# Who makes the sums over k1 beside the convolution: VectorE or GpSimd

## Chip, core and metric

The kernel runs on one core of a Trainium2 chip. The metric is the device time of one execution in microseconds. Engines are named as in the profile: PE (TensorE, matmuls), PEld (its weight loads), DVE (VectorE), ACT (ScalarE), POOL (GpSimd), SP (SyncE, which issues most DMAs).

## What is computed

Two blocks follow each other: a long convolution by FFT with a gate, and a maxout FFN.

```python
h_mlp = np.maximum(pos_emb @ w1, 0.0) @ w2          # filter, S x D
h_filt = h_mlp * np.exp(-0.01 * pos)[:, None]
u = x * v                                           # 4 x 12544 x 128
Uf, Hf = np.fft.rfft(u, n=2*S, axis=1), np.fft.rfft(h_filt, n=2*S, axis=0)
y = np.fft.irfft(Uf * Hf[None], n=2*S, axis=1)[:, :S]
a = x * y                                           # as 50176 tokens x 128
h = np.maximum(np.maximum(a @ moe_w1, a @ moe_w2), a @ moe_w3)   # d_ff 768
return h @ moe_w_out
```

## The kernel before

The FFT over 2S points is written as matmuls with constant tables: a first transform over 90 values of k1, a second stage per pair of k1 (group g, 45 of them), the product with the filter's spectrum, the inverse second stage (back to DRAM, `zd`), and a last transform over k1 that gives y. The FFN works with the differences w2-w1 and w3-w1, so that two relu-like maxima and one folded matrix `lin` give the maxout.

**Passes, tiles and slots.** After a first part that convolves batch 0, there are four FFN passes, one per batch b. Pass b runs over 32 tiles i of 392 tokens; a tile has six slots f, one per 128 columns of d_ff. Slot number s = 6i + f. In each slot `up` (L155 into `hps`, L702 on ACT, L705 on DVE) makes one piece of h, and `down` (L155 into `ops`) of two slots earlier multiplies it by `wo_sb`. `hps` has three PSUM banks in strict turns, and each `up` takes two, so the bank read by L705 of slot s is the one that slot s+2 writes first: L705 has to end by then.

**What is woven in.** Passes 0, 1 and 2 carry the convolution of batch b+1. `conv_steps` lays it out: first the input's transforms (u steps, slots 3 to about 55 or 62), then the pairs. For a group x, two groups at a time, there are: `g_quarter` (PE, L463 for the second stage of g=x, L473 for the inverse one of z=x-3), `g_fold` (ACT L485, DVE L488 twice, out of PSUM), `g_store` (POOL DMA, L496), `q_swap` (ACT L503, L504), `q_re` (DVE L507), `q_im` (DVE L512, then POOL L515), and two `q_unfold` (DVE L519), whose result L473 reads three groups later. Fold, swap and store have fixed slots; `q_re`, `q_im` and `q_unfold` go to the slot with the least load in a short list, `load`, among the few that are allowed. Every engine works through its queue in the order in which the program was written.

**The sums over k1.** For the next tile, `t_load` brings `zt` from `zd` on SP, `t_sums` forms even = z0 + z1 (L670) and z1 = z0 - z1 (L671), and `t_last` transforms both on PE (L155 into `cps`, slot f = 2 to 4) and multiplies by x on DVE (L692, `gt`). `t_sums` stands ahead of `up` in slot f = 0. Which engine it uses is decided there: DVE in a pass's last tile, DVE once the pairs have begun (`i * NF > pairs_from`), POOL before. For the upper half of the tiles of passes 1 to 3 a sign is needed, and `t_sums` takes DVE's scalar_tensor_tensor (L674, L675) whatever engine is named. `pairs_from` is s0, 55 in pass 0 and 62 in passes 1 and 2.

```python
if f == (3 if turn_ else 0):
    t_sums(tiles[n + 1], nc.vector if turn_ or i * NF > pairs_from else nc.gpsimd)
```

Outputs leave by a POOL DMA (L720), in the queue behind what POOL has to do before. Pass 3 has no convolution beside it and sums on DVE; POOL adds products there (L735).

Of the kernel before, what the change touches and what calls it, by code (L numbers as in the profile page):

```python
# [28 lines left out]
LATE = 3  # L29
# [61 lines left out]
def kernel(  # L91
# [15 lines left out]
    nc = tc.nc  # L107
# [4 lines left out]
    NF = DFF // P  # L112
    NK = N1 // 2
# [459 lines left out]
    def conv_steps(b, done):  # L573


        out = []

        def at(slot, late, fn, *args):
            out.append((slot, late, len(out), fn, args))

        per_pair = 170 / (NK + LATE + 0.6 * (NU - done))
        for u in range(done, NU):
            s = (u - done) * 0.6 * per_pair + 9
            at(max(0, int(s) - 9), 0, u_load, b, u)
            at(int(s) - 6, 0, u_mul, u)
            at(int(s) - 5, 0, u_planes, u)
            at(int(s) - 4, 0, u_dma, u)
            at(int(s), 0, u_join, u)  # L590
            at(int(s + 1), 1, u_first, u)
        s0 = int((NU - done - 1) * 0.6 * per_pair + 9) + 6

        def start(x):
            return s0 + int(x // 2 * 2 * per_pair)

        load = [(1.2 if i % NF == 3 else 0.6) + (1.4 if i % NF == 0 and i > s0 else 0)
                for i in range(NT * NF)]
        for x in range(NK + LATE):
            s = start(x)  # L600
            load[s] -= 1.2
            load[s + 1 + x % 2] += 1.4

        def emptiest(among, cost):
            s = min(among, key=lambda i: load[i])
            load[s] += cost
            return s

        for x in range(NK + LATE):
            s, odd = start(x), x % 2  # L610
            g, z = x if x < NK else None, x - LATE if x >= LATE else None
            at(s, 1, g_quarter, g, z)
            at(s + 1 + odd, 0, g_fold, g, z)
            at(s - 4, 0, w_load, x)
            if z is not None:
                at(s + 3 + odd, 0, g_store, b, z)
            if g is None:
                continue
            if g % 2 == 0:
                at(s - 4, 0, q_load, g, min(2, NK - g))  # L620
                at(s - 1, 0, h_load, g, min(2, NK - g))
            first = s + 2 + 2 * odd
            at(first, 0, q_swap, g, 0)
            at(first + 1, 0, q_swap, g, 64)
            last = start(x + LATE) - 1
            a = emptiest(range(first + 1, min(first + 3, last - 1) + 1), 0.7)
            at(a, 0, q_re, g)
            a = emptiest(range(a, min(first + 4, last - 1) + 1), 0.7)
            at(a, 0, q_im, g)
            for q in range(2):  # L630
                at(emptiest(range(a + 1, last + 1), 0.55), 0, q_unfold, g, q)
        slots = {}
        for s, _, _, fn, args in sorted(out, key=lambda r: r[:3]):
            slots.setdefault(s, []).append((fn, args))
        return slots, {start(x) + 1 for x in range(NK + LATE)}, s0


    N = 4 * NB
    NT = P // 4
    zts, xTs, gs, pos_, obs = ({} for _ in range(5))  # L640

    def t_load(b, i):
        zt = hp.tile([N1, 2, 512], FP32, tag="zt", name="zt", bufs=2)
        for c in range(2):
            if b == 0:
                nc.sync.dma_start(
                    zt[NK * c:NK * c + NK],
                    zd[b].rearrange("(g a) c t f -> g a c t f", a=2)[
                        :, :, c, 2 * i:2 * i + 2, :].rearrange("g a t f -> g a (t f)"))
                continue  # L650
            q, j = divmod(i, NT // 2)
            for a in range(2):
                nc.sync.dma_start(
                    zt[NK * c:NK * c + NK, a].rearrange("g (t f) -> g t f", t=2),
                    zd[b].rearrange("(g a) c t q f -> g a c t q f", a=2)[
                        :, a, c ^ (a & q), 2 * j:2 * j + 2, q, :])
        zts[b, i] = zt[:, 0], zt[:, 1]
        if i % 2:
            return
        xT = hp.tile([D, 2, 4, NB], FP32, tag="xT", name="xT", bufs=2)  # L660
        for c in range(GC):
            nc.sync.dma_start(xT[c * NG:(c + 1) * NG].rearrange("d i p n -> d (i p) n"),
                              x[:, 4 * i:4 * i + 8, c, b, :])
        xTs[b, i], xTs[b, i + 1] = xT[:, 0], xT[:, 1]

    def t_sums(i, eng=nc.gpsimd):
        z0, z1 = zts[i]
        even = hp.tile([N1, 512], FP32, tag="even", name="even", bufs=2)
        if i[0] == 0 or i[1] < NT // 2:
            eng.tensor_tensor(out=even[:], in0=z0, in1=z1, op=ALU.add)  # L670
            eng.tensor_tensor(out=z1, in0=z0, in1=z1, op=ALU.subtract)  # L671
        else:
            for out, op in ((even[:], ALU.add), (z1, ALU.subtract)):
                nc.vector.scalar_tensor_tensor(out=out, in0=z1, scalar=sign_t[:, 0:1], in1=z0,  # L674
                                               op0=ALU.mult, op1=op)  # L675
        zts[i] = even[:], z1

    def t_last(i):
        zt = zts.pop(i)
        ps = state["bank"]()  # L680
        own = i[0] == B - 1 and i[1] > 1
        g = (lp if own else hp).tile([D, 4, NB], FP32, tag="g", name="gt", bufs=4 if own else 3)
        y = ps[:, 0:N].rearrange("d (p n) -> d p n", p=4)

        h = NB // 2
        for s in range(4):
            for a in range(2):
                halves_mm(y[:, s, a * h:a * h + h], zt[a][:, s * D:(s + 1) * D],
                          f4p[:, i[0] > 0 and i[1] >= NT // 2, a, :], s == 0 and a == 0, True)
        y = y.rearrange("d p (a m) -> d p m a", a=2)  # L690
        xT = xTs.pop(i)
        nc.vector.tensor_tensor(out=g[:].rearrange("d p (m a) -> d p m a", a=2), in0=y,  # L692
                                in1=xT.rearrange("d p (m a) -> d p m a", a=2),
                                op=ALU.mult)
        gs[i] = g

    def up(i, f, tag="hid", bufs=3):
        rhs = gs[i][:].rearrange("d p n -> d (p n)")
        h = (hidp if tag == "hid" else lp).tile([P, N], FP32, tag=tag, name="hid", bufs=bufs)
        pa = next(hbanks)  # L700
        halves_mm(pa[:, 0:N], w_sb[1][:, f * P:(f + 1) * P], rhs, True, True)
        nc.scalar.activation(h[:], pa[:, 0:N], Relu)  # L702
        pb = next(hbanks)
        halves_mm(pb[:, 0:N], w_sb[2][:, f * P:(f + 1) * P], rhs, True, True)
        nc.vector.tensor_tensor(out=h[:], in0=h[:], in1=pb[:, 0:N], op=ALU.max)  # L705
        return h
# [108 lines left out]
    def run(steps):  # L815
        for fn, args in steps:
            fn(*args)
# [147 lines left out]
    EARLY = 6  # L965
# [73 lines left out]
    tiles = [(b, i) for b in range(B) for i in range(NT)]  # L1039
    LAST = (B - 1) * NT  # L1040
    late = []
    for n, (b, i) in enumerate(tiles[:LAST]):
        if i == 0:
            beside, folds, pairs_from = conv_steps(b + 1, EARLY if b == 0 else 0)
        if n == 0:
            t_load(*tiles[0])
            t_load(*tiles[1])
            t_sums(tiles[0], nc.vector)
            t_last(tiles[0])
        for f in range(NF):  # L1050

            if i < NT - 2:
                if f == 0:
                    t_load(*tiles[n + 2])
            elif i == NT - 1 and f < 2 and n + 1 + f < len(tiles):
                t_load(*tiles[n + 1 + f])
            turn_ = i == NT - 1
            if f == 0:
                when = 4 if turn_ else min((3, 4, 2), key=lambda k: i * NF + k in folds)
            if f == (3 if turn_ else 0):  # L1060
                t_sums(tiles[n + 1], nc.vector if turn_ or i * NF > pairs_from else nc.gpsimd)
            if f == 4 and n + 1 == LAST:
                t_sums(tiles[n + 2], nc.vector)
            h = up((b, i), f)
            late.append(((b, i), f, h))
            if len(late) > 2:
                down(*late.pop(0))
            if f == when:
                t_last(tiles[n + 1])
            if f == 5 and n + 1 == LAST:  # L1070
                t_last(tiles[n + 2])
            s = i * NF + f
            run(beside.pop(s, ()))
            if s == NT * NF - 1:
                assert not beside, sorted(beside)
# [26 lines left out]
    step, b = 0, B - 1  # L1102
    for i in range(0, NT, 2):
        h = {}
        X, Y = banks if i % 4 == 0 else banks[::-1]
        for j, (name, f) in enumerate(ORDER):
            n = int(name[1]) - 1
# [64 lines left out]
```

## Time and profile before

| | |
|---|---|
| time, median of 3 runs | 2317.72 us (2315.53 to 2319.48) |
| profiled execution | 2315.53 us, of it the span 2313.7 us |
| pass 0 | about 326 to 846 us of the span |
| passes 1 and 2 | about 846 to 1375 and 1375 to 1900 us |
| pass 3 | from about 1900 us |
| pairs in pass 0, 484 to 846 us | PE busy 359.8 of 362 us, DVE 277.2, ACT 214.4, POOL 110.7 |
| DVE L488, L507, L512, L519, one | 0.65, 0.68, 0.68, 0.42 us |
| POOL L515, one | 1.27 us |

In the timeline a row gives the start in us from the span's start, the duration, engine, line, operation, output and inputs, shapes and the number of merged instructions; in square brackets stand the engine's idle time before it and what ended that. In the list of waits the three numbers are the total in us, the number of times and the longest. In a tile's rows they are the shortest, median and longest duration in ns, then the first and last start. Durations of neighbours overlap by some 0.1 us, as an engine starts an instruction while the one before it drains.

### The profile page before, as it was taken

To read this page: it belongs to the slowest core of one execution; us is meant where nothing else is said; L and a number is where in the kernel's file an instruction comes from. 1 tells how busy PE (TensorE), PEld (TensorE's weight loads), DVE (VectorE), ACT (ScalarE), POOL (GpSimd) and SP (SyncE) were. 2 spreads that over 40 slices of the span, in tenths; PEclk is the share of its full clock that TensorE was granted. 3 is DMA by queue.
4 is the path that set the end of the run, shared out by engine and by line. 5 is a ranking of instruction groups with operands and counts; after the bars stand their busy time and mean duration, and the time that the engine had idled before them with its cause. 6 is when DMAs were issued, how large, how long until landed. Compare 5 with 4: busy or idle time off the path is not lost.

```text
span 2313.7 us, 68365 instructions
## 1 busy us (share of the span) xinstructions
PE 2277.5 (98%) x27853; PEld 1379.8 (60%) x27853; DVE 1574.2 (68%) x2856; ACT 1177.5 (51%) x2124; POOL 898.8 (39%) x1095
## 2 busy tenths in 40 slices
PE   8999989999999999999999999999999999999998
PEld 7989866655555546655555446655555546666665
DVE  5678856667887847757888847758888854445443
ACT  2678844446666624446666634446666632222222
POOL 1045424413333324423333333423333326666666
PEclk9999999999999999999999999999999999999999
DMA  7869959979998849979999849969999832222221
GB/s 158 206 202 266 290 155 189 166 172 246 232 244 216 210 119 192 185 147 242 248 243 250 214 120 189 186 144 247 247 246 240 225 91 56 54 56 71 65 55 22
DMA packets 473148, 410.95 MB, mean 178 GB/s; under 512 B 328004, under 2 KB 374231, under 8 KB 472834
## 3 DMA queue, kind: packets, MB, share of 16 engines
q1 hardware_dynamic: 433714, 317.68, 62.4%
q0 software_dynamic: 26400, 75.72, 11.2%
q10 hardware_dynamic: 12720, 13.18, 1.8%
q8 instruction: 219, 3.59, 0.7%
q14 instruction: 95, 0.78, 0.1%
HBM read 262.77 MB, written 84.67 MB: 150 GB/s over the span
## 4 chain that ended last, share of the span: by engine, by line
PE 84%; DMA 6%; ACT 3%; DVE 3%; issue 2%; SPq 1%; ACTq 1%; POOL 0%; DVEq 0%; POOLq 0%
PE hps L155 41%; PE ops L155 17%; PE ops L765 6%; PE cps L409 5%; PE cps L155 4%; PE cps L463 3%; PE ps L164 3%; PE cps L473 2%; DMA ht<-hd 2%; PE last L155 1%; DMA hd<-ht 1%; ACT ht L958 1%; DMA wt<-wq_const 1%; PE pm L324 1%; DMA zt<-zd 1%
## 5 line engine op out<-in xcount | busy, mean ns | idle before, releaser
L155 PE MATMUL hps<-gt,w_sb 128*64 128x392 f32 x6144 | 1150.4, 495 | 6.1 <-DVE hid L705 5.3
L702 ACT ACTIVATE hid<-hps 128x392 f32<-128x392 f32 x768 | 383.9, 500 | 736.6 <-PE hps L155 720.7
L155 PEld LDWEIGHTS hps<-gt,w_sb 128*64 128x64 f32 x6144 | 424.5, 137 | 437.4 <-issue 391.3
L705 DVE TENSOR_TENSOR hid<-hid,hps 128x392 f32<-128x392 f32 x768 | 427.3, 557 | 333.6 <-PE hps L155 323.9
L155 PE MATMUL ops<-hid,wo_sb 128*64 128x392 f32 x2304 | 478.6, 492 | 0.0
L515 POOL TENSOR_TENSOR cb<-cb,xs 128x512 f32<-128x512 f32 x135 | 181.7, 1346 | 471.4 <-DVE xs L512 331.1
L155 PEld LDWEIGHTS ops<-hid,wo_sb 128*64 128x64 f32 x2304 | 169.0, 137 | 210.2 <-issue 210.2
L488 DVE TENSOR_TENSOR cb<-cps,eo 128x512 f32<-128x512 f32 (+1 forms) x288 | 175.1, 649 | 65.6 <-ACT eo L485 65.1
L420 DVE TENSOR_TENSOR spec<-cps,high 128x360 f32<-128x360 f32 x180 | 135.5, 794 | 121.9 <-ACT high L418 121.9
L720 POOL DMA_DIRECT2D out_dram<-ot x96 | 74.9, 781 | 354.2 <-ACT ot L718 301.8
L503 ACT ACTIVATE xs<-cb 32x512 f32<-32x512 f32 x270 | 169.6, 628 | 22.8 <-DVE cb L488 14.3
L504 ACT COPY xs<-cb 32x512 f32<-32x512 f32 x270 | 166.3, 616 | 3.1
L418 ACT COPY high<-cps 128x360 f32<-128x360 f32 x90 | 71.9, 799 | 152.5 <-PE cps L409 125.8
L519 DVE TENSOR_TENSOR xs<-cb 128x256 f32<-128x256 f32 x270 | 141.8, 568 | 7.5 <-POOL cb L515 7.5
L409 PEld LDWEIGHTS cps<-f1q,uT 98*64 98x64 f32 x2880 | 124.9, 137 | 30.6 <-issue 30.6
L409 PE MATMUL cps<-f1q,uT 98*64 98x90 f32 x2880 | 128.1, 241 | 0.4 <-DVE uT L393 0.4
L378 POOL COPY planes<-ut 128x784 uint16<-128x784 uint16 x90 | 75.7, 841 | 111.1 <-DVE ut L357 110.2
L496 POOL DMA_DIRECT2D zd<-cb x135 | 92.5, 687 | 61.9 <-DVE cb L488 54.0
L155 PEld LDWEIGHTS cps<-f4p,even 90*64 90x64 f32 x1568 | 89.8, 139 | 38.4 <-issue 34.7
L155 PE MATMUL cps<-f4p,even 90*64 90x49 f32 x1568 | 96.5, 221 | 2.8 <-DVE even L670 2.8
L155 PE MATMUL cps<-f4p,zt 90*64 90x49 f32 x1568 | 97.8, 223 | 0.3 <-DVE zt L671 0.3
L507 DVE TENSOR_TENSOR cb<-cb,ht 128x512 f32<-128x512 f32 x135 | 92.0, 682 | 7.7 <-ACT xs L504 7.1
(137 smaller groups left out, 3205.9 us busy)
## 6 DMA issues: line engine op xcount, KB each, us to landing
ht<-hd SPq DMA_DIRECT2D x264, 256.0 KB, 6.8
wt<-wq_const SPq DMA_DIRECT2D x144, 256.0 KB, 6.4
zd<-cb POOLq DMA_DIRECT2D x135, 256.0 KB, 6.1
zt<-zd SPq DMA_DIRECT2D x384, 90.0 KB, 3.0
sq<-spec SPq DMA_DIRECT2D x264, 128.0 KB, 7.3
ut<-in_xr_dram SPq DMA_DIRECT2D x128, 196.0 KB, 4.2
ut<-in_vr_dram SPq DMA_DIRECT2D x128, 196.0 KB, 4.5
xT<-in_x_dram SPq DMA_DIRECT2D x256, 98.0 KB, 3.5
```

The source lines that it names most:

```text
L155: nc.tensor.matmul(out[64 * h:64 * h + 64], lhsT[:, 64 * h:64 * h + 64], rhs, start=start, stop=stop, skip_group_check=True)
L409: nc.tensor.matmul(ps[64 * c:64 * c + 64, 256 * i + h * N1:256 * i + (h + 1) * N1], t[:, 2 * ((at + i) % 8) + h].rearrange("n r t -> n (r ...
L420: nc.vector.tensor_tensor(out=spec[:, :, a, at:at + n], in0=v[:, 1], in1=high, op=op)
L488: nc.vector.tensor_tensor(out=cb[:, a, lo:hi], in0=ps[:, lo:hi], in1=eo[:, lo:hi], op=op)
L496: nc.gpsimd.dma_start(zd[b][2 * z:2 * z + 2].rearrange("k c t a f -> (k c t) a f"), zss.pop(z))
L503: nc.scalar.mul(xs[at:at + 32], xt[at + 32:at + 64], -1.0)
L504: nc.scalar.copy(xs[at + 32:at + 64], xt[at:at + 32])
L515: nc.gpsimd.tensor_tensor(out=xts[g], in0=xts[g], in1=xs[:], op=ALU.add)
L519: nc.vector.tensor_tensor(out=ab[:, q], in0=y[:, 0], in1=y[:, 1], op=(ALU.subtract, ALU.add)[q])
L702: nc.scalar.activation(h[:], pa[:, 0:N], Relu)
L705: nc.vector.tensor_tensor(out=h[:], in0=h[:], in1=pb[:, 0:N], op=ALU.max)
L765: nc.tensor.matmul(ps[64 * c:64 * c + 64, 0:H2], w, rhs[:, H2 * c:H2 * c + H2], start=start, stop=True, skip_group_check=True)
```

## The change

The condition on `pairs_from` goes, so that all sums that name an engine, but those in a pass's last tile, are made on POOL. `load`, which sets the places of `q_re`, `q_im` and `q_unfold`, counts sums on DVE in the slots f = 0 only where they need a sign, from slot 96 on in passes 1 and 2.

```diff
-        load = [(1.2 if i % NF == 3 else 0.6) + (1.4 if i % NF == 0 and i > s0 else 0)
+        load = [(1.2 if i % NF == 3 else 0.6) + (1.4 if i % NF == 0 and b > 1 and i >= NT * NF // 2 else 0)
                 for i in range(NT * NF)]
...
-        return slots, {start(x) + 1 for x in range(NK + LATE)}, s0
+        return slots, {start(x) + 1 for x in range(NK + LATE)}
...
-            beside, folds, pairs_from = conv_steps(b + 1, EARLY if b == 0 else 0)
+            beside, folds = conv_steps(b + 1, EARLY if b == 0 else 0)
...
-                t_sums(tiles[n + 1], nc.vector if turn_ or i * NF > pairs_from else nc.gpsimd)
+                t_sums(tiles[n + 1], nc.vector if turn_ else nc.gpsimd)
```

In `conv_steps` b is the batch that is convolved, one more than the pass. In pass 0 the placements change in slots 84 to 86, 90, 91, 95, 96, 132 to 134, 138, 139, 143 and 144; in passes 1 and 2 in slots 90 and 91 alone: single `q_unfold`, `q_re` or `q_im` steps move by one slot.

## The prediction

> **What bounds the kernel now.** The page first: TensorE is busy in 98% of the span, at the full granted clock in every slice but the first.
>
> ```profile
> span 2313.7 us, 68365 instructions
> PE 2277.5 (98%) x27853; PEld 1379.8 (60%) x27853; DVE 1574.2 (68%) x2856; ACT 1177.5 (51%) x2124; POOL 898.8 (39%) x1095
> ```
>
> The change takes no matmul away, so it can only touch the moments in which PE waits. The waits of PE come next:
>
> ```profile
> PE hps L155 <- DVE hid L705: 5.3, 10, 0.9
> PE cps L473 <- DVE gt L692: 0.5, 1, 0.5
> ```
>
> All waits for VectorE's relu maxima are 5.3 us in ten places. In the timeline four of them (start of the waiting matmul 567.59, 583.72, 695.45, 711.58) lie in the first FFN pass beside pairs, behind sums that move; 1103.02 and 1625.02 belong to sums with a sign (L674), which stay. The tile's rows say what there is to move, and what it costs on either engine:
>
> ```profile
> L670 DVE TENSOR_TENSOR even<-zt x48: 676/679/1592, 326.4 to 2058.4; 90x512 f32<-90x512 f32 x48
> L670 POOL TENSOR_TENSOR even<-zt x32: 1262/1272/1452, 330.4 to 1530.8; 90x512 f32<-90x512 f32 x32
> L671 DVE TENSOR_TENSOR zt<-zt x48: 686/688/1653, 327.2 to 2059.1; 90x512 f32<-90x512 f32 x48
> L671 POOL TENSOR_TENSOR zt<-zt x32: 1263/1274/1614, 331.8 to 1532.2; 90x512 f32<-90x512 f32 x32
> ```
>
> Medians 0.68 and 0.69 us on DVE, 1.27 each on POOL. The maxima, over twice the medians, say that something blocks some of them.
>
> **What moves.** Pass 0 gives POOL the sums made in tiles 10 to 30 (21 pairs), passes 1 and 2 those in tiles 11 to 14 (4 each): 29 pairs, which agrees with 32 L670 already on POOL (10+11+11) and with the two programs' order (58 rows move; PE, ACT and SP keep theirs). DVE loses 29 x 1.37 = 39.7 us, POOL gains 29 x about 2.6 = 75 us. Neither total is on the path: PE waits for single late instructions.
>
> **The gain.** At slot 84 (tile 14) DVE does two folds, the two sums, then the maximum that frees PE's bank:
>
> ```profile
> 564.46 1.29 DVE L488 TENSOR_TENSOR cb<-cps,eo 128x512 f32<-128x512 f32 x2 [1.22 <-ACT eo L485]
> 565.66 0.68 DVE L670 TENSOR_TENSOR even<-zt 90x512 f32<-90x512 f32 x1
> 566.37 0.69 DVE L671 TENSOR_TENSOR zt<-zt 90x512 f32<-90x512 f32 x1
> 566.98 1.02 DVE L705 TENSOR_TENSOR hid<-hid,hps 128x392 f32<-128x392 f32 x2
> ```
>
> and PE, in the same stretch:
>
> ```profile
> 566.34 0.83 PE L155 MATMUL ops<-hid,wo_sb 128*64 128x392 f32 x4
> 567.59 1.54 PE L155 MATMUL hps<-gt,w_sb 128*64 128x392 f32 x8 [0.42 <-DVE hid L705]
> ```
>
> A group of four matmuls takes 0.66 us to issue (564.36 to 565.02 just before), so PE would have gone on at 567.00 and starts at 567.59: 0.59 us lost (0.42 of it shown as idle). Without the sums L705 follows the folds, 1.3 us sooner, and the wait goes; next late would be L705 of the following slot, which has over 2 us to spare (end 568.01; its bank is used again at 570.27. Spare time is meant so from here on). Tiles 15, 22 and 23 look the same: 4 x 0.59 = 2.4 us. POOL does these sums early: its last pair addition ends at 560.67, zt landed at 551.64, and until 563.3 DVE runs only L488 and L705, which read one input from PSUM.
>
> The other wait of pass 0, L473 at 813.28 (0.47 idle), stays: the chain to it passes an L507 that waited until 808.53 for ACT's L504, not for the sums.
>
> **The cost.** POOL and DVE block each other when both read SBUF; first DVE's timeline, then POOL's:
>
> ```profile
> 612.10 0.68 DVE L670 TENSOR_TENSOR even<-zt 90x512 f32<-90x512 f32 x1
> 612.82 1.64 DVE L671 TENSOR_TENSOR zt<-zt 90x512 f32<-90x512 f32 x1
> ```
>
> ```profile
> 612.42 1.49 POOL L515 TENSOR_TENSOR cb<-cb,xs 128x512 f32<-128x512 f32 x1 [6.52 <-ACT hid L702]
> ```
>
> L671 takes 1.64 instead of 0.69, ending 0.55 after L515; L515 had first waited for L670 (1.49 instead of 1.27). So DVE instructions with two SBUF inputs (L507, L512, L519) stand still under a POOL addition; L705 and L488 don't. And the two alternate: L515 at 585.11 took 1.70 and let one L519 through, then held the second.
>
> So each pair of sums is looked at by what DVE does then. POOL runs it right behind the L515 or store before it. In 18 of the 29 tiles folds and maxima follow: no collision. Eleven have unfoldings (L519) there. Passes 0 (tiles 17, 18, 25, 26) and 1, 2 (tile 12): L507, L512 or an L519 come up to 1 us later, while the next L705 has 1.5 to 3.6 us to spare and the quarter matmuls get their operand in time: nothing, up to 0.3 each. The same new wait sits in front of whatever follows on DVE's queue, L705 first, hence the slack above. POOL's own queue (L515, store L496, output L720) moves by up to 2.6 us; the unfolding that needs the L515 comes two or more slots (over 5 us) later there.
>
> Tiles 16 and 24 pay, because the quarter transform reads the last unfolding at once:
>
> ```profile
> 596.97 0.68 DVE L512 TENSOR_TENSOR xs<-xs,ht 128x512 f32<-128x512 f32 x1
> 600.33 0.74 DVE L519 TENSOR_TENSOR xs<-cb 128x256 f32<-128x256 f32 x2
> ```
>
> ```profile
> 600.80 0.78 PE L473 MATMUL cps<-xs,wt 64*64 64x128 f32 x16
> ```
>
> L473 already follows the unfoldings closely (0.78, elsewhere 0.62). After the change one L519 moves behind L705 (the emptier slot 96), so L512 ends at 597.3 and L515 runs 597.5 to 598.8. Then, in turns: L519 done 599.05, first sum to 600.3, second L519 600.6, second sum to 601.9, third L519 602.2. L473's second half started at about 601.13 and now starts at 602.1 or so: 0.95 us, twice: 1.9 us. Bounds: 0 (POOL keeps out until DVE is through) to 1.3 each (both sums ahead of all three).
>
> Tile 10 of pass 0 and tile 11 of passes 1 and 2 are ties: DVE's unfolding waits for the L515 itself (L519 at 500.64, 0.03 after L515's end at 500.61), while POOL's next instruction is stamped 0.05 before the end of the one in front (L496 613.86, L515's end 613.91). But a POOL stamp is not yet its hold: at 585.11 and 585.26 DVE came 0.15 later and still ran. So DVE gets through first, the second unfolding after the first sum, at 502.5, and L473 (start 502.17, second half 502.5) loses under 0.1. Bounds 0 to 1.1 each if POOL takes it first; I take 0, since the two stamps are nearer than 0.15.
>
> [...]
>
> **Moved placements.** The new load list shifts a few L519, L507 and L512 by one slot, among them one L519 into slot 90 of passes 1 and 2, 0.33 us ahead of an L705 with 3.07 us to spare: nothing.
>
> **The sum.** -2.4 + 1.9 = -0.5 us, on the profiled run's 2315.5 (span 2313.7 and 1.8 around it), that is 2317.2 from the median 2317.7. 0.2% is 4.6 us, about what a measurement of this kernel can tell from no change.
>
> **Rivals.**
> (a) POOL takes ties and keeps the ports through both sums. Then tiles 10, 16, 24 of pass 0 and tile 11 of passes 1 and 2 hold L473 for 1.2 to 1.45 us: 5 x 1.3 = 6.5, minus 2.4: +4.1. If the four tiles 18, 26, 12, 12 lose their last unfolding too (L473 there starts 629.99, the unfolding would end at 631.6: 1.6 each), +6.4: +10.5, 2328. It decides from the moment that a fifth tile is lost: +4.7 is slower by this measure. For it: POOL's stamps come first. Against: the L519 at 585.26. Taken at +6.5: 2324.2. Chance 0.30.
> (b) Relief is worth more: every wait of pass 0 that DVE has a hand in goes (4 x 0.59, 0.65 at 813, two of 0.22 before quarter matmuls, two of 0.24 at tiles 16 and 24, all worked out from the issue pitch like the 0.59: 3.9 us) and nothing is paid: 2313.8. Even this is under 4.6. Chance of more than that 0.06.
> (c) The ties alone go to POOL, +3.2: 2320.4; it counts as no change.
> That the change does nothing is excluded by the moved rows; that its effects cancel is the forecast, 0.64 with (c).
>
> **Range.** From (b), 2313.8, to (a) with one more tile, 2325: the cases between hold 8 in 10.
>
> **What would show it.** After: L670 and L671 19 times each on DVE, 61 on POOL; no PE wait near 567, 583, 695, 711; waits for DVE's maxima down from 5.3 to about 3.6; new waits of L473 for L519 of about 1 us near 601 and 728, none near 502, 1038 and 1561. DVE busy about 35 us less. Wrong would be L519 of 2.6 us (both sums ahead) or PE waits at ten places.

## The result

The changed kernel takes 2327.08 us (median of 4 runs, 2326.81 to 2328.18) against 2316.97 us (4 runs) for the kernel before beside it: a ratio of 1.0043, interval 1.0026 to 1.0061. That is 10 us slower, outside the predicted range, and near the high end of rival (a) (+10.5). The profiled run took 2326.81 us, 11.3 more than the profiled run of before. One of the ten runs of the control `b0_plain_copy` below took 4763.66 us, in a slower state, and is left out there. Some lines of the page, and then of PE's list of waits (total us, times, longest):

```profile
span 2325.0 us, 68379 instructions
PE 2282.1 (98%) x27853; PEld 1378.6 (59%) x27853; DVE 1551.9 (67%) x2798; ACT 1178.9 (51%) x2124; POOL 967.3 (42%) x1153
```

```profile
PE cps L473 <- DVE xs L519: 7.5, 9, 1.0
PE hps L155 <- DVE hid L705: 3.3, 6, 0.6
PE cps L473 <- DVE gt L692: 3.0, 1, 3.0
```

The waits for DVE's maxima fell from 5.3 to 3.3 us (forecast: about 3.6). In their place stands a line that before did not have: nine waits of L473 for L519, 7.5 us. And the one wait for L692 grew from 0.5 to 3.0. Together these are waits of PE at ten places, which the prediction had named as a sign of being wrong.

**Where it lies.** The distance from the first `up` matmul of one tile to that of the next, after minus before, puts the whole difference into a few tiles. Pass 3 is equal within 0.01 us; the passes before it grew by 7.58, 1.88 and 1.89 us, of which 0.50 in tile 0 of pass 0 comes ahead of any moved sum.

| tiles | tile length, after minus before, us |
|---|---|
| pass 0, tiles 14, 15, 22, 23 | -0.64 each |
| pass 0, tiles 13 and 21; tile 14 of passes 1 and 2; tile 15 of pass 1 | -0.1 each; -0.35 in the last |
| tile 10 of pass 0; tile 11 of passes 1 and 2 (the ties) | +1.25; +0.91, +0.46 |
| pass 0, tiles 16 and 24 | +0.78, +0.77 |
| pass 0, tiles 18 and 26; tile 12 of passes 1 and 2 | +1.50, +1.53; +1.37, +1.51 |
| pass 0, tile 29 | +4.06 |

The gains are 3.3 us, the ten losses 14.1. Together with the 0.5 that is the 11.3 of the profiled runs.

**A tie.** The timelines of DVE, POOL and PE in tile 10, each row with its start, duration, engine and line:

```profile
501.09 2.88 DVE L519 TENSOR_TENSOR xs<-cb 128x256 f32<-128x256 f32 x2 [0.97 <-POOL cb L515]
```

```profile
499.79 1.27 POOL L515 TENSOR_TENSOR cb<-cb,xs 128x512 f32<-128x512 f32 x1 [9.10 <-DMA zt<-zd]
501.03 1.26 POOL L670 TENSOR_TENSOR even<-zt 90x512 f32<-90x512 f32 x1
502.37 1.33 POOL L671 TENSOR_TENSOR zt<-zt 90x512 f32<-90x512 f32 x1
```

```profile
502.63 0.45 PE L473 MATMUL cps<-xs,wt 64*64 64x128 f32 x8
504.03 0.45 PE L473 MATMUL cps<-xs,wt 64*64 64x128 f32 x8 [0.95 <-DVE xs L519]
```

DVE starts 0.065 us after L670's stamp and loses: its first unfolding takes 1.48 us instead of 0.42, and so does its second, behind L671. Two unfoldings take 2.88 us, and L473's second half waits 0.95.

**Behind a store.** Tile 18 in the kernel before, DVE and then POOL:

```profile
626.97 2.07 DVE L519 TENSOR_TENSOR xs<-cb 128x256 f32<-128x256 f32 x3
```

```profile
626.83 1.26 POOL L515 TENSOR_TENSOR cb<-cb,xs 128x512 f32<-128x512 f32 x1 [5.42 <-DVE xs L512]
628.04 0.68 POOL L496 DMA_DIRECT2D zd<-cb  x1
```

and the three timelines of tile 18 after the change:

```profile
627.60 0.55 DVE L705 TENSOR_TENSOR hid<-hid,hps 128x392 f32<-128x392 f32 x1
628.07 4.63 DVE L519 TENSOR_TENSOR xs<-cb 128x256 f32<-128x256 f32 x3
```

```profile
627.82 1.26 POOL L515 TENSOR_TENSOR cb<-cb,xs 128x512 f32<-128x512 f32 x1 [5.33 <-ACT hid L702]
629.04 0.67 POOL L496 DMA_DIRECT2D zd<-cb  x1
629.65 1.36 POOL L670 TENSOR_TENSOR even<-zt 90x512 f32<-90x512 f32 x1
631.09 1.33 POOL L671 TENSOR_TENSOR zt<-zt 90x512 f32<-90x512 f32 x1
```

```profile
632.76 0.45 PE L473 MATMUL cps<-xs,wt 64*64 64x128 f32 x8 [0.95 <-DVE xs L519]
```

The three unfoldings take 4.63 us; in before they took 2.07, beside the same L515. One by one they are 1.31 (beside L515), 2.00 and 1.48 us. The second is the surprise: it is stamped 629.30, 0.35 us ahead of the first sum's stamp, while POOL is at a store, and yet it doesn't end until 631.30, after that sum. DVE was shut out before the sum had begun by its own record. The store alone does not do this: in before the second and third unfolding begin beside it (628.30 and 628.63) and take 0.41 us each.

**Tile 29.** The same happens with the sums that tile 30 makes for tile 31. They stand in the program ahead of slot 180, but POOL's queue holds nothing between the last store and them, so POOL runs them four slots early (at 815.25, when DVE is at slot 176; PE reaches slot 180 at 825.39), straight behind the last group's L515 and store. The unfoldings again take 4.63 us; this time L692, which frees PE's bank, queues behind them. First PE's timeline; then stretches, with their length, the busy time of the five engines PE, PEld, DVE, ACT and POOL, the granted clock as a share of full speed (1.00, 0.50, 1.00 here), the DMA share and GB/s:

```profile
819.30 1.13 PE L473 MATMUL cps<-xs,wt 64*64 64x128 f32 x16 [3.04 <-DVE gt L692]
820.36 2.56 PE L155 MATMUL hps<-gt,w_sb 128*64 128x392 f32 x8
823.41 1.48 PE L155 MATMUL hps<-gt,w_sb 128*64 128x392 f32 x8
```

```profile
818.00:819.00 1.00, 0.00 (x0) 0.00 (x0) 1.00 (x3) 0.00 (x0) 0.02 (x1) 1.00 0.00 0
820.00:821.00 1.00, 1.00 (x11) 0.32 (x8) 0.00 (x0) 0.00 (x0) 0.00 (x0) 0.50 0.06 16
823.00:824.00 1.00, 1.00 (x8) 0.42 (x6) 0.96 (x3) 0.00 (x0) 0.00 (x0) 1.00 0.00 0
```

After 3.04 us without a matmul PE came back at half its clock (819.05 to 822.46): eight matmuls took 2.39 us to issue (820.36 to 822.75) instead of 1.32 (823.41 to 824.73). The 4.06 us are 3.04, less the 0.47 that were there before, and some 1.5 for the slow clock.

### The profile page after: what moved, and what is told of

Read it like the earlier page. It is cut to its first block, busy times and chain, and to the rows that moved or that the text cites. A ratio compares the mean times of both kernels' runs of the same rounds, so it can differ in the third digit from the quotient of the medians.

```text
span 2325.0 us, 68379 instructions
## 1 busy us (share of the span) xinstructions
PE 2282.1 (98%) x27853; PEld 1378.6 (59%) x27853; DVE 1551.9 (67%) x2798; ACT 1178.9 (51%) x2124; POOL 967.3 (42%) x1153
## 4 chain that ended last, share of the span: by engine, by line
PE 82%; DMA 5%; DVE 5%; issue 3%; ACT 3%; SPq 1%; ACTq 0%; POOL 0%; DVEq 0%; POOLq 0%
PE hps L155 40%; PE ops L155 16%; PE ops L765 6%; PE cps L409 5%; PE cps L155 4%; PE ps L164 3%; PE cps L473 2%; PE cps L463 2%; DVE xs L519 2%; PE last L155 1%; DMA ht<-hd 1%; DMA hd<-ht 1%; ACT ht L958 1%; PE pm L324 1%; PE pst L362 1%
## 5 line engine op out<-in xcount | busy, mean ns | idle before, releaser
L515 POOL TENSOR_TENSOR cb<-cb,xs 128x512 f32<-128x512 f32 x135 | 176.2, 1305 | 452.9 <-DVE xs L512 207.1
L519 DVE TENSOR_TENSOR xs<-cb 128x256 f32<-128x256 f32 x270 | 167.2, 661 | 9.8 <-POOL cb L515 9.8
L507 DVE TENSOR_TENSOR cb<-cb,ht 128x512 f32<-128x512 f32 x135 | 93.3, 691 | 8.1 <-ACT xs L504 7.6
L789 POOL DMA_DIRECT2D out_dram<-o x128 | 77.4, 610 | 49.8 <-DVE o L782 48.1
```

The source lines that it names most:

```text
L507: nc.vector.tensor_tensor(out=xts[g], in0=xts[g], in1=hts[g][:, 0].rearrange("p k q d -> p q k d"), op=ALU.mult)
L515: nc.gpsimd.tensor_tensor(out=xts[g], in0=xts[g], in1=xs[:], op=ALU.add)
L519: nc.vector.tensor_tensor(out=ab[:, q], in0=y[:, 0], in1=y[:, 1], op=(ALU.subtract, ALU.add)[q])
```

## The experiments

All of them, the two controls too, read the convolution's input with a plain DMA copy of the same bytes where the kernels before and after use a DMA that turns it; the turning is left out. Their line numbers are larger by one or more (the unfolding is L520, its quarter matmul L474, the sums L671, L673 or L674). Ratios are to the kernel before, run beside them. Tile lengths are now the run's minus those of `b0_plain_copy`. "Port" in the prediction, the expectations and below is the author's name for what one of the two engines holds while the other stands still: the runs show which instruction stands still beside which and for how long, no run shows a port. The ten places with a loss are named `HIT` in the edits:

```python
HIT = {(0, 10), (0, 16), (0, 18), (0, 24), (0, 26), (0, 30),
       (1, 11), (1, 12), (2, 11), (2, 12)}      # (pass, tile that makes the sums)
```

**Controls.** `b0_plain_copy` is the kernel before and `a0_plain_copy` the kernel after, with that copy alone.

```diff
-        nc.sync.dma_start_transpose(
-            out=t[:], in_=us.pop(u)[:].rearrange("p h s n -> p (h s n)"))
+        nc.sync.dma_start(
+            out=t[:].rearrange("p a b -> p (a b)"),
+            in_=us.pop(u)[:].rearrange("p h s n -> p (h s n)"))
```

> The kernel before, but the DMA that turns the batch's planes is a plain copy of the same bytes (the turning is left out, the outputs of batches 1 to 3 change). It is the base of the variants below, which all have it. The turned planes are needed long before the pairs begin, so both theories say 2315 to 2319, within 2 us of the kernel before.

> The changed kernel with the same plain copy in place of the turning DMA. Both theories: 10 us above the base b0, as 2327.1 stands above 2317.0 (9 to 11.5).

Measured: 2319.13 us (1.0006, 0.9996 to 1.0016) and 2328.05 us (1.0042, 1.0028 to 1.0057). The copy changes nothing that matters here, and the loss is there between the two: 11.2 us by the tiles' lengths, 8.9 by the medians. Three tiles with moved sums differ from the table above by more than 0.3 us. Tile 29 loses 5.17: the wait is about the same (3.05 us), but PE is slow for longer behind it. The eight matmuls took 2.67 us to issue (822.11 to 824.78; 2.39 in the kernel after), and the record of the next two is 0.87 us long, where two take 0.50 at the full clock. Tile 11 of pass 1 loses nothing against b0, because in b0 PE waits there for 0.63 us for a table's load (`wt`). Such waits for loads stand in single tiles of several profiles, and a tile's length has to be read with them in mind.

The third is tile 17, which lost nothing in the kernel after and loses 0.65 in a0. It is a tie of a second kind: the first unfolding waits for the L515, and POOL has a store and then the sums behind that L515. DVE in the kernel after, then DVE and POOL in a0:

```profile
614.72 2.18 DVE L519 TENSOR_TENSOR xs<-cb 128x256 f32<-128x256 f32 x2 [0.41 <-POOL cb L515]
```

```profile
615.82 3.60 DVE L520 TENSOR_TENSOR xs<-cb 128x256 f32<-128x256 f32 x2 [0.41 <-POOL cb L516]
```

```profile
615.73 0.69 POOL L497 DMA_DIRECT2D zd<-cb  x1
616.35 1.38 POOL L671 TENSOR_TENSOR even<-zt 90x512 f32<-90x512 f32 x1
```

In a0 the first unfolding is stamped 0.52 us ahead of the sum and is shut out all the same (2.19 us); in the kernel after, stamped 0.53 ahead, it ran in 0.43. Tiles 17 and 25 have this tie in eight kernels whose sums there are on POOL without a gate (after, a0, e1c, e3c, e4c, e6, e7, e9): the unfolding comes 0.03 us after the end of the L515 and 0.52 to 0.54 ahead of the sum's stamp, gets through 13 times of 16 and is shut out three times.

**The halves of the change.** `e1c_engine_only` moves the sums and keeps the old load list; `e2c_load_only` takes the new list and leaves the sums on DVE.

```diff
 e1c (on after)
-(1.4 if i % NF == 0 and b > 1 and i >= NT * NF // 2 else 0)
+(1.4 if i % NF == 0 and i > s0 else 0)
 e2c (on before): the same line the other way round
```

> Plain copy; the sums on POOL as in the change, the load list of before. Port theory: the list matters little, so it stays 8 to 11 us above b0. In tiles 16 and 24 one L519 more stands ahead of L515, so these two lose less (0.3 to 0.8 each); tiles 14, 15, 22, 23 keep their gain. Rival, placements: the loss comes from the steps that the new list puts into the slots of the sums, then it falls back to b0.

> Plain copy; the load list of the change, the sums on DVE as before. Port theory: within 1.5 us of b0. Rival, placements: most of the 10 us.

Measured: 2328.16 us (1.0051, 1.0035 to 1.0066), and 2317.57 us (0.9999, 0.9989 to 1.0008). The engine makes the loss; the list by itself changes nothing that the interval can tell. Of e1c's expectation tiles 16 and 24 missed: they lose 0.92 each, not 0.3 to 0.8. In e2c they lose 0.22 each, so the moved unfolding is not free there, but with the sums on POOL the old places are the worse ones.

**The ten places, put back.** `e4c_mixed` makes the sums of `HIT` on DVE again (and counts them in `load`); `e3c_tile30_on_dve` only those of tile 30.

```diff
-t_sums(tiles[n + 1], nc.vector if turn_ else nc.gpsimd)
+t_sums(tiles[n + 1], nc.vector if turn_ or (b, i) in HIT else nc.gpsimd)        # e4c
+t_sums(tiles[n + 1], nc.vector if turn_ or (b, i) == (0, 30) else nc.gpsimd)    # e3c
```

> Plain copy; sums back on DVE only in the ten places that collided (pass 0 tiles 10, 16, 18, 24, 26, 30, passes 1 and 2 tiles 11 and 12), counted in the load list; the other 19 pairs stay on POOL. Port theory: the ten losses (14.1 us by the tiles' lengths) go, the gains (4 x 0.64 and about 0.7) stay: a0 less 13 to 14, about 3 us faster than b0. Rival, POOL's queue is late everywhere: the loss falls in proportion, a0 less 3.5. Rival, the gains are not real: equal to b0.

> The changed kernel (plain copy), with only the sums made in tile 30 of pass 0 back on DVE, one pair of 29. By the tiles' lengths tile 29 lost 4.06 us: POOL runs these sums four slots early, onto three unfoldings, then L692 and the quarter bank are late, and PE runs its next matmuls at half pace. Port theory (the loss comes from ten places where POOL's sums and DVE's L519 want the same read port): a0 less 4.1 (3.5 to 4.5). Rival, the loss is spread over POOL's longer queue: a0 less 10/29 = 0.35.

Measured: e4c 2314.95 us (0.9987, 0.9978 to 0.9997). The nineteen other pairs stay on POOL and their gains remain (-0.64 four times), and of the waits of L474 for L520 one of 0.3 is left. (Tile 10 is 1.74 longer than in b0 even so; PE waits there for 1.51 us for a load of `wt`.) e3c took 2322.80 us (1.0021, 1.0012 to 1.0030), 5.2 below a0, and tile 29 is 0.09 shorter than in b0: one misplaced pair of sums is worth half of the whole loss. The expected 4.1 was too little, since in a0's profile that tile had lost 5.17 against b0.

**Is it POOL's reading?** `e5_pool_writes_only` puts six fills of the same tiles in place of each of the 29 pairs, with no read of SBUF.

```diff
-            eng.tensor_tensor(out=even[:], in0=z0, in1=z1, op=ALU.add)
-            eng.tensor_tensor(out=z1, in0=z0, in1=z1, op=ALU.subtract)
+            if write_only:
+                for _ in range(3):
+                    nc.gpsimd.memset(even[:], 0.5)
+                for _ in range(3):
+                    nc.gpsimd.memset(z1, 0.5)
```

> Plain copy; the changed kernel, but beside the pairs the 29 pairs of sums are replaced by POOL instructions that only write the same two tiles, three fills of 90 x 512 f32 for each (the sums are left out, the outputs are not the reference's). POOL stays busy at the same places, for 1 to 4 us per pair (the length of such a fill is not in any trace), but reads nothing. Read-port theory: no L519 above 1.5 us, no PE wait of L473 for L519, total as e4 (2313.5 to 2316). Rival, POOL's queue: what stands behind the sums (L515, stores, outputs) is late as in the change, 2322 or more. Rival, DVE and POOL also fight over writing: L519 stays long.

Measured: 2313.80 us (0.9982, 0.9973 to 0.9992). POOL's and then DVE's timeline in tile 18:

```profile
629.46 1.26 POOL L516 TENSOR_TENSOR cb<-cb,xs 128x512 f32<-128x512 f32 x1 [5.31 <-ACT hid L711]
630.67 0.68 POOL L497 DMA_DIRECT2D zd<-cb  x1
631.25 1.80 POOL L675 MEMSET even<- 90x512 f32 x3
633.00 1.68 POOL L677 MEMSET zt<- 90x512 f32 x3
```

```profile
629.70 1.97 DVE L520 TENSOR_TENSOR xs<-cb 128x256 f32<-128x256 f32 x3
632.07 0.68 DVE L508 TENSOR_TENSOR cb<-cb,ht 128x512 f32<-128x512 f32 x1
```

POOL is busier than with the sums (3.4 us against 2.7), the three unfoldings take 1.97 us, and L508, wholly beside the fills, takes 0.68. All ten losses are gone. So it is neither POOL's time nor its place in the queue, but its reading of SBUF.

**Is it when POOL reads?** `e6_gate` keeps the reads and all 29 pairs on POOL, but in the ten places lets POOL begin only when DVE has passed a point behind its unfoldings: DVE fills a one-column flag and POOL overwrites it, which makes POOL wait for DVE. In four tiles the sums also move behind the pairs' steps of the slot.

```diff
+    LATER = {(0, 16), (0, 24), (1, 11), (2, 11)}
+    def gate():
+        nc.vector.memset(flag[:], 0.0)
+        nc.gpsimd.memset(flag[:], 0.0)
...
+            late_sums = (b, i) in LATER
-            if f == (3 if turn_ else 0):
+            if f == (3 if turn_ else 0) and not late_sums:
+                if (b, i) in HIT:
+                    gate()
                 t_sums(tiles[n + 1], nc.vector if turn_ else nc.gpsimd)
...
+            if f == 0 and late_sums:
+                gate()
+                t_sums(tiles[n + 1])
```

> Plain copy; the changed kernel with all sums on POOL, but in the ten colliding places POOL may start them only when DVE has done the unfoldings of that place: DVE fills a one-column tile behind them, POOL fills the same tile ahead of the sums and so waits. In pass 0 tiles 16 and 24 and in tile 11 of passes 1 and 2 the sums stand behind slot 0's steps for that. Theory of moments (it is not the POOL work but when it runs): the ten losses go, L507 or L512 get up to 1.6 us longer instead, in front of maxima with 2 us and more to spare: 2314 to 2316.5. Rival, any 2.6 us of POOL reading costs the same wherever it lies: 2325 or more.

Measured: 2312.99 us (0.9980, 0.9970 to 0.9990). The ten losses are gone. Tiles 17 and 25, the ties of the second kind, have no gate in e6; here both go against DVE (2.18 us for the first unfolding) and lose 0.65 each. In tile 18 POOL still shuts DVE out, later and where nothing waits (DVE's timeline):

```profile
627.61 1.98 DVE L520 TENSOR_TENSOR xs<-cb 128x256 f32<-128x256 f32 x3
629.52 0.55 DVE L714 TENSOR_TENSOR hid<-hid,hps 128x392 f32<-128x392 f32 x1
629.53 0.06 DVE L684 MEMSET flag<- 128x1 f32 x1
629.99 1.61 DVE L508 TENSOR_TENSOR cb<-cb,ht 128x512 f32<-128x512 f32 x1
631.53 1.75 DVE L513 TENSOR_TENSOR xs<-xs,ht 128x512 f32<-128x512 f32 x1
```

L508 and L513 take 1.61 and 1.75 us instead of 0.68, and PE doesn't notice. Here a collision costs only where PE needs the result, or what stands behind it on DVE, at once.

**When does POOL take the port?** By the stamp of the sum it can't be (tiles 17 and 18). Two theories were open: one instruction ahead of the sum (the hand-over of e7's expectation), or as soon as POOL's last reader in front of it is done (theory A of e9's). `e7_spacer` puts one fill of 128x128 ahead of the sums in the ten places, `e9_long_fill` two of 128x512.

```diff
+                if (b, i) in HIT:
+                    nc.gpsimd.memset(spare[:], 0.0)      # e7: spare 128x128, once; e9: 128x512, twice
                 t_sums(tiles[n + 1], nc.vector if turn_ else nc.gpsimd)
```

> Plain copy; the changed kernel with one short POOL fill (128 x 128 f32, writes only, an estimated 0.15 to 0.25 us from the 0.52 us of 512 columns) ahead of the sums in the ten colliding places. It tests how far ahead of its stamp POOL takes the read port. Theory hand-over (the next POOL instruction takes the port as soon as the one in front of it is under way, that is one instruction ahead): with the fill in front, the sums can't take it while L515 or L496 run; in tile 10 and tiles 11 the first unfolding gets through at 0.4 us instead of 1.48, as I had predicted for the change, and L473 loses 0 to 0.2 there; in tiles 18, 26, 12, 12 the second unfolding gets through and one is held instead of two: these fall from 1.5 to 0.3 or less. Total a0 less 5 to 9. Rival, POOL's queue holds the port however deep the reader stands in it: only the 0.2 us shift, a0 within 1.5.

> As e7_spacer, but with two GpSimd fills of a 128x512 tile (about 0.52 us each, from the fills of e5_pool_writes_only) ahead of the sums in the ten places instead of one of 0.2 to 0.3 us. Theory A: POOL's next instruction that reads SBUF takes the port as soon as the last reader before it on its queue (L515) has ended, and only fills between the two put this off; the store between them does not. Then the hold begins some 1.04 us after the L515 before it instead of at once: in tile 18 of pass 0 near 629.7, when the third unfold subtraction has ended (about 629.2), so none of the ten places loses anything that PE waits for; 2312 to 2316 us, a0_plain_copy less 12 to 15. In tile 29 of pass 0 the wait of 3.0 us for gt is gone. Theory B: a POOL instruction that waits in the queue with its conditions met bars VectorE however many instructions that don't read stand before it: then the ten losses stay, as in e7_spacer, near 2328 us, and tile 10 loses as it did or more. Theory C: it is the start of POOL's instruction by its stamp that counts: the fills move the stamp by 1.04 us past all three subtractions in every place, so this can't be told from A here; e7_spacer speaks against it already.

Measured: e7 2328.26 us (1.0043, 1.0030 to 1.0057). The ties came out as expected: in tile 10 the sum's stamp now lies 0.08 after DVE's, the first unfolding takes 0.43 us (0.42 in both tiles 11), and the loss falls from 1.25 to 0.20. Behind a store nothing is won, though (18 and 26 lose 1.68 and 1.65, tile 29 4.20), and 16 and 24 stay at 0.78, so the expectation for the whole missed; the total, 0.2 above a0, is that of its rival. POOL and DVE in tile 18 of e7:

```profile
627.43 1.27 POOL L516 TENSOR_TENSOR cb<-cb,xs 128x512 f32<-128x512 f32 x1 [5.32 <-ACT hid L705]
628.66 0.68 POOL L497 DMA_DIRECT2D zd<-cb  x1
629.25 0.31 POOL L1066 MEMSET spare<- 128x128 f32 x1
629.41 1.38 POOL L673 TENSOR_TENSOR even<-zt 90x512 f32<-90x512 f32 x1
```

```profile
627.68 4.81 DVE L520 TENSOR_TENSOR xs<-cb 128x256 f32<-128x256 f32 x3
```

The second unfolding, stamped 628.92, is now 0.50 ahead of the sum's stamp and is still shut out (2.17 us). The stamps therefore don't decide it. The fill puts the sum's stamp 0.14 us later (0.71 after L516's end instead of 0.56 in a0), and its own record is 0.24 us long (median of the ten). Counted from L516's end at 628.71 that gives 628.85 to 628.95, just before the first unfolding makes way at 628.99; so theory A allows the hold, by a margin under 0.15 us.

e9: 2313.08 us (0.9984, 0.9975 to 0.9994), 15.0 below a0. The same place, POOL and then DVE:

```profile
624.26 1.27 POOL L516 TENSOR_TENSOR cb<-cb,xs 128x512 f32<-128x512 f32 x1 [5.32 <-ACT hid L705]
625.47 0.68 POOL L497 DMA_DIRECT2D zd<-cb  x1
626.06 1.21 POOL L1067 MEMSET spare<- 128x512 f32 x2
627.24 1.44 POOL L673 TENSOR_TENSOR even<-zt 90x512 f32<-90x512 f32 x1
```

```profile
624.51 1.97 DVE L520 TENSOR_TENSOR xs<-cb 128x256 f32<-128x256 f32 x3
626.40 0.55 DVE L708 TENSOR_TENSOR hid<-hid,hps 128x392 f32<-128x392 f32 x1
626.88 0.68 DVE L508 TENSOR_TENSOR cb<-cb,ht 128x512 f32<-128x512 f32 x1
627.48 1.76 DVE L513 TENSOR_TENSOR xs<-xs,ht 128x512 f32<-128x512 f32 x1
```

The three unfoldings are through (1.97 us), the ten places lose nothing for which L474 waits, and the wait of 3.04 us is gone. (Tile 12 of pass 2 is still 0.84 longer than in b0, that of pass 1 0.25; PE's idle time there, 0.61 and 0.44, is for a table's load, `wt`.) Theory B as it is worded, that fills in front change nothing, fails here and already in the ties of e7. In one point e9 is not what theory A, taken literally, says: the port should have been gone 1.04 after L516's end, at 626.57, but L508 at 626.88 ran undisturbed in 0.68 us, and the sum waited for it (1.44 us instead of 1.27). The reason was not shown. Against e7 it changes two things at once, the fill's length and that a second one writes the same tile, and no run separates them.

**The best version.** `e8_gate12` is e6 with `LATER` extended by `(0, 17)` and `(0, 25)`, so that the two tiles with a tie of the second kind are gated as well.

```diff
-    LATER = {(0, 16), (0, 24), (1, 11), (2, 11)}
+    LATER = {(0, 16), (0, 17), (0, 24), (0, 25), (1, 11), (2, 11)}
```

> Plain copy; e6 with two more gates, in tiles 17 and 25 of pass 0, where the first gate kernel lost 0.65 us each against b0 (L473 0.42 idle for an unfolding behind a sum). Theory of moments: e6 less 1.3, about 2311.7, 5 to 6 below b0's and the kernel before's runs. Rival: the sums now hold L507 and L512 of these tiles and the fold behind them, equal to e6 or up to 1 us slower.

Measured: 2312.71 us (0.9978, 0.9968 to 0.9987), about 5 us faster than the kernel before and 15 than a0. By tile lengths tiles 17 and 25 are back to nothing, and pass 0 is 3.24 us shorter than in b0, against 1.91 in e6: the 1.3 that was expected. The medians of e6 and e8, each taken beside its own runs of before, differ by 0.3 only. As the two ties can go either way, the runs of e6 need not all hold both losses; one profile of e6 can't show it.

## Why the prediction was wrong

**What held.** The bound, the 29 pairs, 61 and 19 sums on POOL and DVE, DVE's waits near 567, 583, 695 and 711 (gone, 2.56 us by tile length for a term of 2.4). Tiles 16 and 24: the alternation came as worked out, the third unfolding ended at 602.17 (predicted 602.2), and the cost was 1.55 for a term of 1.9. DVE's busy time fell by 22 us, not about 35: what it no longer adds it now spends shut out. That tiles 17 and 25 cost nothing in the kernel after was luck: their first unfolding was as close as 0.53 us ahead of the sum's stamp, and with the same order of work a0 lost 0.65 in tile 17 and e6 in both. One reading of the page was off and carries no weight: the clock is not full in every slice but the first (0.91 over 289 to 347 us), but it is from 484 to 846 us, beside the pairs of pass 0.

**What failed**, in the order of size:

1. "Passes 0 (tiles 17, 18, 25, 26) and 1, 2 (tile 12) ... nothing, up to 0.3 each." Tiles 18, 26 and the two tiles 12 cost 5.9 us. The unfoldings were to come "up to 1 us later"; in tile 18 the three took 4.63 us instead of 2.07, so the last came 2.56 later, and PE waited 0.95 for it. The step took the sum's stamp behind the store as the first moment of a hold, which puts the second unfolding ahead of it. Rival (a) had this price (1.6 each; measured 1.37 to 1.53).
2. "In 18 of the 29 tiles folds and maxima follow: no collision." It placed tile 30's sums at their slot in the program; POOL ran them four slots earlier, beside unfoldings. 4.06 us, and in no rival. A queue that runs ahead has to be followed to what it really runs beside.
3. "DVE gets through first ... I take 0" for the three ties. They cost 2.62 us. DVE lost at 0.065 us after the sum's stamp. The step rested on a single row, the unfolding at 585.26 that ran 0.15 after POOL's stamp, and the same trace has more of them: in before, 32 unfoldings are stamped 0.145 to 0.156 us after an L515 that POOL began after idling for 1 us or more; 8 run at once and 24 are shut out (so in tile 18: 626.97 against 626.83, 1.40 us for the first). Nor do the stamps give the order the other way round: in tile 18 of the kernel after the unfolding stamped 0.35 us ahead of the sum was the one shut out.

-0.5 plus 5.9, 4.1 and 2.6, less 0.35 at tiles 16 and 24 and 0.9 of further gains, is +10.8: the measured difference of the tiles.

**What stands behind the second unfolding.** Behind a store an unfolding was barred 0.35 us ahead of the sum's stamp (after), and in three cases of 16 even 0.52 to 0.53 ahead, 0.03 after the end of the L515; behind a store and a short fill 0.50 ahead (e7). L508 was not barred 0.36 ahead where two fills stand in front (e9). So the hold can begin about where POOL's last reader ends, and the store in between doesn't put it off. What in POOL lets the sum shut DVE out while the store still runs was not shown by any run.

## What to carry to other kernels

Before work moves to GpSimd because VectorE is busy, list for each moved instruction what VectorE does with two SBUF inputs from the end of GpSimd's previous SBUF reader on, not from the stamp, and whether PE reads that result at once: here 19 of 29 places cost nothing, two of them by luck, and ten cost four times what all gave. Don't read the order of two engines off one row when their stamps lie as close as 0.15 us; count how the trace's other rows of that kind went. Place it by where GpSimd's queue will run it, which may be slots ahead of where it is written. If it collides, let GpSimd wait for VectorE there: twelve such waits (e8) cost PE nothing that shows and turned 10 us lost into about 5 us won.

## What the hardware showed that was not expected

- GpSimd can shut VectorE's two-input instructions out 0.35 to 0.53 us before the stamp of its reading instruction when a store of 0.68 us stands in front. After idling, on the contrary, it let 8 of 32 unfoldings through that were stamped 0.145 to 0.156 us after it, and shut out 24 (before).
- Fills by GpSimd (0.52 us for 90x512 f32, 0.19 to 0.31 for 128x128) didn't disturb VectorE's two-input instructions, even back to back for 3.4 us: L508 beside them took 0.68 us (e5), the median of L507 in before.
- At the end of a wait of 3.04 us PE's granted clock was half (1.00 in 818 to 819, 0.50 in 820 to 822), for 3.4 us in the kernel after: with the slow matmuls behind it the stall of 3 us costs 4.5 there and 5.6 in a0.
